# A fused sliding-window attention and GELU MLP: the first MLP product of the last two token tiles with half its columns as seven block products

## The chip, the core and the metric

The kernel runs on one core of a Trainium2 chip. The metric is the device time of one execution in microseconds; several runs are made, and their median is the time of the kernel. The engines are named as in the profile: PE is TensorE, DVE is VectorE, ACT is ScalarE, POOL is GpSimd, SP is SyncE (which here only issues transfers).

## What is computed

```python
# q, k, v: (8 batches, 8 heads, 576 positions, 64), float32
scores = (q @ k.T) / 8                      # only |i - j| <= 32 kept
x = (softmax(scores) @ v)                   # as (4608 tokens, 512)
h = x @ w_in                                # w_in: (512, 2048)
g = 0.5 * h * (1 + tanh(sqrt(2/pi) * (h + 0.044715 * h**3)))
out = g @ w_out                             # w_out: (2048, 512), result float32
```

## The kernel before

The attention output is kept in SBUF, transposed and in fp16, as `xT`: 128 partitions x 4 blocks of the 512 model columns x a ring of 1536 tokens. The MLP runs over 9 tiles `t` of 512 tokens (line 816). The attention of batch `b = t + 1` is worked in between the matmuls of tile t, so tiles 7 and 8 have no attention of their own, but for the tail of batch 7 in tile 7.

**First product** (`ffn_in`, line 525). For each of 16 columns of 128 hidden units, four matmuls of 128 x 128 weights by 512 tokens add up in one PSUM bank; `gelu` (line 550) sends the bank through the GELU on ScalarE into `gTs[t]` (fp16). The call number n is mapped to a column by `column`: n = 0, 1, 2, 3 are columns 0, 8, 1, 9, and so on. After every fourth n, `sums` (line 579) forms on VectorE four sums S1 to S4 of the GELU outputs (columns 2i, 2i + 1 with columns 8 + 2i, 9 + 2i, and the two halves of the tokens), which the second product needs. `S2` needs `S1`, `S4` needs `S2`. The first three columns of a tile are begun (three of four matmuls) at the end of the tile before (lines 930 to 932).

**Second product** (`ffn_out`, line 625). For t of 1 and up the product with `w_out` is already a Strassen-Winograd one: `WINO` (line 41) lists seven products, each of 16 matmuls of 256 columns, 112 in all, numbered i = 0 to 111. Product 0 is A11 B11 and goes over f = 0 to 7, one f for each GELU column of the lower half; product 1 is S2 T2. At the end of each product VectorE copies a bank out or adds it to what was kept (lines 653 to 671), and `ffn_last` makes the last sum; `store` issues the output, mostly on GpSimd's queue. Some products add into a bank that has just been copied out, so TensorE waits for that copy.

**Order of the work.** Every engine takes its instructions in the order in which the program issues them. The attention is placed by hand: a plan (`PLAN`, line 46, for tiles 2 to 6; `PLAN_0` and `PLAN_1` for tiles 0 and 1) says at which i which steps are visited: `s` scores and exponential, `m` the mask on VectorE, `v` the sums and the product with V and the inversion on ScalarE (with the load of a tail of V on GpSimd's queue at `v-1`), `x` the product into `xT` on VectorE; `@` names the PSUM pair, and -1 is the tail of the batch before. Ahead of the first visit ScalarE's table is loaded anew. Tile 7 has `v-1` at 5 and `x-1` at 31. `load_v` and a one-column copy that waits for the transposed keys are issued on GpSimd's queue at i = 4.

**PSUM.** Eight banks: `psM` has two (`bank(0)`, `bank(1)`), `psS` two pairs (`S0`, `S1`), `psO` two (`O`, `D`). The first product of tiles 1 and up uses banks 0 and 1, `D`, and for n = 1, 2 the pair `S0`. The tail's weights at `v-1` of tile 7 use `O` and `D`, and `D` is also the bank of n = 15.

**Copies touched.** At the end of tile 0, `ffn_out_0` (line 612) copies four banks out, those of t4 = 0, 1 on VectorE, t4 = 2, 3 on ScalarE (line 622). In tile 1 the block C11 is copied out by ScalarE, in later tiles by VectorE (line 657).

Of the kernel before, what the change touches and what calls it, by code (L numbers as in the profile page):

```python
# [9 lines left out]
FP32 = mybir.dt.float32  # L10
FP16 = mybir.dt.float16
AF = mybir.ActivationFunctionType
ALU = mybir.AluOpType
# [23 lines left out]
def cut(b):  # L37
# [5 lines left out]

PLAN = {4: "s0@0 s1@1 v-1", 16: "m0 m1 x-1", 33: "s2@0 v0@1 v1", 36: "m2", 44: "x0", 50: "x1",
        62: "s3@0 s4@1 v2", 66: "m3", 80: "x2", 84: "m4", 91: "v3", 112: "x3"}


# [4 lines left out]
          29: "w2", 33: "s-1@1 n0@0", 35: "e0", 36: "m2", 37: "k3", 38: "w5", 39: "m-1", 40: "r3@1", 43: "e1",  # L54
          46: "s3@0 v-1@1 d0", 47: "w3 e2", 48: "d1 m3", 51: "n2@0", 52: "e3 d2 d3 x-1",
          55: "u3 p0@0 p2@1 x0 x1", 56: "e4 x2 x3", 60: "c1"}
PLAN_1 = {12: "s0@0 s1@1 s2", 16: "m0 m1", 36: "m2", 45: "v0@1 v1 s-1@0", 52: "x0", 55: "x1", 62: "m-1",
          69: "s3@0 v2 v-1@1", 73: "m3", 81: "x2", 85: "x-1", 91: "v3 s4@1", 112: "x3 m4"}
PAIR_1 = {17: slice(0, 4), 40: slice(4, 8)}
# [10 lines left out]
def kernel(  # L70
# [479 lines left out]
    def gelu(t, n):  # L550
        fc = column(t, n)
        nc.scalar.activation(gTs[t][:, fc, :], phs[fc], AF.Gelu_apprx_tanh)  # L552
        if t and n % 4 == 3:
            sums(t, n // 4)

    wino = {}

    def combine_w():
# [53 lines left out]
    def ffn_out_0(t4, fc):  # L612
        new = t4 not in pys
        if new:
            pys[t4] = bank(t4) if t4 < 2 else psO.tile([128, 512], FP32, name="py3", tag="OD"[t4 % 2])
        nc.tensor.matmul(pys[t4], gTs[0][:, fc, t4 * 128:t4 * 128 + 128], w_out16[:, fc, :],
                         start=new, stop=(fc == NF - 1))
        if fc == NF - 1:
            if "yo" not in pys:
                pys["yo"] = hp.tile([128, 2, 512], FP32, name="yo2", tag="qt16")  # L620
            yo = pys["yo"][:, t4, :] if t4 < 2 else yp.tile([128, 512], FP32, name="yo", tag="yo")
            (nc.scalar.copy if t4 > 1 else nc.vector.tensor_copy)(yo, pys[t4])  # L622
            later.append((t4, yo))

    def ffn_out(t, i):

        n, blk, f = i // 16, i // 8 % 2, i % 8
        a, w, new = WINO[n]
        end = t == NT - 1
        if i % 16 == 0 and new:  # L630
            pys[n % 2] = bank((1 + n) % 2)
            if end and n == 4:
                pys["apart"] = psO.tile([128, 512], FP32, name="py2", tag="O")
        py = pys[n % 2].rearrange("p (b c) -> p b c", b=2)
        apart = end and blk and n in (4, 6)
        if a[0] == "A":
            r0, c0 = 8 * (int(a[2]) - 1) + f, 256 * (int(a[1]) - 1) + 128 * blk
            lhsT = gTs[t][:, r0, c0:c0 + 128]
        else:
            lhsT = wino[a][:, f, 128 * blk:128 * blk + 128]  # L640
        one = end and n in (4, 6)
        nc.tensor.matmul(pys["apart"][:, 0:256] if apart else py[:, blk, :], lhsT,  # L642
                         wino[w][:, f, :], start=(new and i % (8 if one else 16) == 0),
                         stop=(i % (8 if one else 16) == (7 if one else 15)),
                         skip_group_check=True)
        if i % 16 < 15:
            return
        yo, left, right = wino["yo"], slice(0, 256), slice(256, 512)
        C11, C12, C21, C22 = (yo[:, r:r + 2, c] for r in (0, 2) for c in (left, right))

        M1, U2, U3 = C21, C12, C22
        if n == 0:
            nc.vector.tensor_copy(M1, py)
        elif n == 1:
            nc.vector.tensor_tensor(U2, py, M1, op=ALU.add)
        elif n == 2:
            (nc.vector.tensor_copy if t > 1 else nc.scalar.copy)(C11, py)  # L657
            if end:
                for x in range(2):
                    store(t, x, yo[:, x, :], left, nc.sync)  # L660
        elif n == 3:
            nc.vector.tensor_tensor(U3, py, M1, op=ALU.add)
        elif n == 4:
            if not end:
                nc.vector.tensor_tensor(C22, py, U3, op=ALU.add)
            else:
                for x, part in enumerate((py[:, 0, :], pys["apart"][:, 0:256])):
                    nc.vector.tensor_tensor(C22[:, x, :], part, U3[:, x, :], op=ALU.add)
                    store(t, 2 + x, yo[:, 2 + x, :], right, nc.sync, nc.scalar)
        elif n == 5:  # L670
            nc.vector.tensor_tensor(C21, py, M1, op=ALU.add)  # L671
            for x in range(2):
                store(t, 2 + x, yo[:, 2 + x, :], *((left, nc.sync, nc.scalar) if end else ()))
# [142 lines left out]
    for t in range(NT):  # L816
        b = t + 1
        att = b < B
        if t:
            for fc in range(begun):  # L820
                ffn_in(t, fc, 3, 4, then=False)
            for fc in range(begun):
                gelu(t, fc)
            if att and b > 1:
                parts = cast_and_turn(b)
            for fc in range(begun, NF):
                ffn_in(t, fc)
                if t == 1 and fc == 3:
                    parts[0]()
                    combine(4, nc.vector)  # L830
                if t == 1 and 6 <= fc < 10:
                    cast_v(2, fc - 6)
                if t == 1 and 9 <= fc < 14:
                    parts[1](fc - 9)
                if t == 1 and fc == 8:
                    trans_tails(1, psO.tile([128, 8, 128], FP16, name="pt", tag="O"))
                if t == 2 and fc in (8, 9):
                    store(0, *later[1 if fc == 8 else 3])
                if t > 1 and fc == 8 and att:
                    pair_v(b, nc.vector.tensor_copy)  # L840
# [10 lines left out]
        for i in range(113 if t else 65):  # L851
# [3 lines left out]
            for act in plan.get(i, "").split():  # L855
# [8 lines left out]
                elif kind == "e":  # L864
                    cast_vt(1) if g == 4 else cast_v(1, g)
                elif kind == "k":
                    cast_early(1, g, (nc.vector, nc.vector))
                    if g == 2:
                        cast_tails(0, nc.gpsimd, even)
                elif kind == "t":  # L870
                    trans_tails(0, spare(at)[0], even)
                elif kind == "r":
                    trans_pair(1, g, *spare(at), copy=nc.scalar.copy if g == 2 else nc.vector.tensor_copy)
                elif kind in "np":
                    pair = psS.tile([128, 2, 512], FP32, name="ps_od", tag=f"S{at}")
                    for x in range(2):
                        if kind == "n":
                            sum_up(1, g + x, pair[:, x, :], groups[(1, g + x)])
                        else:
                            ods[g + x] = (pair[:, x, :], lts[g + x])  # L880
                            times(1, g + x, pair[:, x, :], groups.pop((1, g + x)))
                    if kind == "n":
                        n = size(1, g)
                        lts[g], lts[g + 1] = lt4[:, g, :], lt4[:, g + 1, :]
                        for x in range(2):
                            nc.scalar.activation(lts[g + x][:, 0:n], pair[:, x, 0:n], AF.Ln)
                        for x in range(2):
                            nc.scalar.activation(lts[g + x][:, 0:n], lts[g + x][:, 0:n], AF.Exp, scale=-1.0)
                elif kind == "u":
                    cast_w(wo[g], w_out16[:, 12:16, :], on_act=(3,), cs=(2, 3))  # L890
                    cast_tails(1, nc.gpsimd)
                    load_qk(2)
                elif kind == "c":
                    if g == 1:
                        B12 = combine_w()
                    combine(g, nc.vector)
                elif kind == "s":
                    score(*group(g), at)
                    if t == 1 and g == 4:
                        load_table(gelu_set)  # L900
                elif kind == "d":
                    pair_chunk(b, g, nc.vector.tensor_copy)
                elif kind == "m":
                    mask(*group(g))
                elif kind == "v":
                    bb, gg = group(g)
                    o, d = weigh(bb, gg, at)
                    ods[g] = (o, invert(bb, gg, d))
                    if t and g < 0 and b + 1 < B:
                        load_vt(b + 1)  # L910
                    if t > 1 and g == (3 if att else -1):
                        load_table(gelu_set)
                else:
                    spread(*group(g), *ods[g])
            if t == 1 and i == 30:
                cast_vt(2)
                store(0, *later[0])
# [43 lines left out]
```

## Time and profile before

| what | value |
|---|---|
| time, three runs | 300.5, 301.97, 308.7 us; median 301.97 |
| time of the profiled execution | 301.21 us |
| its span | 299.5 us |
| granted TensorE clock, mean | 0.998 |
| busy: PE, DVE, ACT, POOL | 287.0, 194.4, 194.1, 91.0 us |
| first product of tile 7 | 242.29 to 256.12 us of the span |
| second product of tile 7 | 256.12 to 269.10 us |
| first product of tile 8 | 269.10 to 282.91 us |

A row of groups gives line, engine, operation, output and inputs with their shapes, the count, the busy time in us, the mean in ns, and the idle time of the engine ahead of it with its releaser. A row of the timeline gives start and duration in us. The chain of waits follows the work that ended last back through what released it; there the matmuls stand one behind the other at the pace at which they are issued[...].

### The profile page before, as it was taken

Reading aid. Unit: us, or ns where it says so; the run is one execution under the profiler, and the core shown is the slowest. Engines: PE = TensorE matmul, PEld = TensorE weight load, DVE = VectorE, ACT = ScalarE, POOL = GpSimd, SP = SyncE. Lnnn points to the kernel's source line nnn. Section 1 sums busy time; section 2 is a strip of 40 time slices with the busy share of each in tenths; the row PEclk is TensorE's granted clock in tenths of the full one; section 3 lists DMA queues with packets and bytes.
Section 4 is the critical chain, followed back from the end, with each engine's and each line's share of the span. In section 5 each row is a group of like instructions: output and inputs, shape, how many; then the busy total and the mean of one; then the engine's idle time right before and its main releaser. Section 6 shows DMA issues by size and latency. Waiting matters only on the chain.

```text
span 299.5 us, 7127 instructions
## 1 busy us (share of the span) xinstructions
PE 287.0 (96%) x2893; PEld 179.6 (60%) x2893; DVE 194.4 (65%) x438; ACT 194.1 (65%) x308; POOL 91.0 (30%) x141
## 2 busy tenths in 40 slices
PE   7889999999899999999999999999999999999994
PEld 3534444446674488448854885478547864784583
DVE  4753577898865975867696769766876635442452
ACT  5866767779586786578566956695678666606600
POOL 3435425202656060605080606060700050016000
PEclk9999999999999999999999999999999999999999
DMA  7999999899799979998999996989694031004013
GB/s 221 266 306 382 354 286 239 230 191 205 188 213 216 244 201 178 168 136 211 176 181 151 220 171 154 146 212 174 106 167 51 3 103 39 2 4 138 2 35 105
DMA packets 116519, 50.73 MB, mean 169 GB/s; under 512 B 98008, under 2 KB 110040, under 8 KB 116487
## 3 DMA queue, kind: packets, MB, share of 16 engines
q1 hardware_dynamic: 87428, 37.88, 62.0%
q0 software_dynamic: 27936, 11.35, 25.2%
q10 hardware_dynamic: 1122, 1.06, 1.1%
q8 instruction: 22, 0.36, 0.5%
q14 instruction: 11, 0.08, 0.1%
HBM read 36.70 MB, written 9.44 MB: 154 GB/s over the span
## 4 chain that ended last, share of the span: by engine, by line
PE 64%; DMA 21%; SPq 7%; ACT 4%; DVE 2%; issue 1%; POOL 0%
PE mm L642 28%; PE mm L544 15%; PE ph L544 13%; DMA KT<-k 5%; DMA tr<-in_q_dram 4%; DMA wst<-in_moe_w_in_dram 3%; DMA wst<-in_moe_w_out_dram 3%; SPq L173 3%; DMA kt<-in_k_dram 3%; PE ps_s L435 2%; DMA vr<-in_v_dram 2%; PE ps_d L462 2%; DMA tr<-in_k_dram 2%; SPq L227 2%; PE ps_o L472 2%; SPq L175 1%
## 5 line engine op out<-in xcount | busy, mean ns | idle before, releaser
L544 PEld LDWEIGHTS <-w_in 128*128 128x128 f16 x576 | 56.1, 98 | 66.6 <-issue 0.9
L544 PE MATMUL mm<-xT,w_in 128*128 128x512 f16 x304 | 74.7, 379 | 0.4 <-DVE yo L622 0.4
L552 ACT ACTIVATE gT<-mm 128x512 f16<-128x512 f32 x76 | 45.1, 597 | 39.9 <-PE mm L544 39.2
L544 PE MATMUL ph<-xT,w_in 128*128 128x512 f16 x272 | 68.2, 379 | 0.4 <-POOL w_in L758 0.4
L606 POOL DMA_DIRECT2D out_dram<-y x55 | 32.7, 604 | 87.4 <-DVE y L671 74.4
L642 PEld LDWEIGHTS <-s 128*128 128x128 f16 x512 | 49.6, 98 | 6.8 <-issue 0.8
L587 DVE TENSOR_TENSOR s<-gT 128x512 f16<-128x512 f16 x64 | 27.2, 426 | 32.1 <-ACT gT L552 32.1
L552 ACT ACTIVATE gT<-ph 128x512 f16<-128x512 f32 x68 | 37.9, 600 | 13.3 <-PE ph L544 13.3
L642 PE MATMUL mm<-t,s 128*128 128x256 f16 x376 | 44.9, 273 | 0.7 <-ACT y L657 0.7
L642 PEld LDWEIGHTS <-gT 128*128 128x128 f16 x384 | 36.0, 98 | 6.6
L448 ACT ACTIVATE pe<-ps_s 128x960 f16<-128x960 f32 (+1 forms) x31 | 29.5, 975 | 13.6 <-PE ps_s L435 13.5
L642 PE MATMUL mm<-w_out,gT 128*128 128x256 f16 x256 | 32.8, 273 | 0.0
L95 ACT ACT_TABLE_LOAD x18 | 23.1, 1283 | 2.2 <-issue 1.9
L498 ACT ACTIVATE lt<-lt 128x480 f32<-128x480 f32 (+3 forms) x36 | 21.1, 585 | 1.1
L497 ACT ACTIVATE lt<-ps_d 128x480 f32<-128x480 f32 (+2 forms) x28 | 15.6, 556 | 9.4 <-PE ps_d L462 6.3
L457 DVE TENSOR_TENSOR pe<-pe,band 128x960 f16<-128x960 f16 x28 | 18.3, 668 | 2.7 <-ACT pe L448 2.7
L181 POOL DMA_DIRECT2D V<-in_v_dram x20 | 17.9, 913 | 0.8 <-issue 0.4
L472 PEld LDWEIGHTS <-V 128*64 128x64 f16 x520 | 13.9, 111 | 7.1 <-DVE V L191 2.4
L642 PE MATMUL mm<-t,gT 128*128 128x256 f16 x128 | 16.3, 273 | 0.0
L435 PE MATMUL ps_s<-QT,KT 64*64 64x128 f16 (+3 forms) x576 | 13.5, 216 | 1.3 <-DMA KT<-k 0.5
L853 POOL COPY after<-KL 128x1 f16<-128x1 f16 x5 | 1.7, 339 | 42.5 <-DMA KL<-kt 42.5
L435 PEld LDWEIGHTS <-KT 64*64 64x64 f16 x576 | 10.0, 106 | 7.5 <-issue 3.4
(111 smaller groups left out, 336.7 us busy)
## 6 DMA issues: line engine op xcount, KB each, us to landing
kr<-in_k_dram SPq DMA_DIRECT2D x31, 256.0 KB, 11.4
qr<-in_q_dram SPq DMA_DIRECT2D x6, 1024.0 KB, 8.1
wst<-in_moe_w_in_dram SPq DMA_DIRECT2D x7, 512.0 KB, 8.2
V<-in_v_dram POOLq DMA_DIRECT2D x20, 128.0 KB, 8.5
wst<-in_moe_w_out_dram SPq DMA_DIRECT2D x2, 1024.0 KB, 11.9
wst<-in_moe_w_out_dram SPq DMA_DIRECT2D x4, 512.0 KB
qr<-in_q_dram SPq DMA_DIRECT2D x7, 256.0 KB, 6.8
out_dram<-y POOLq DMA_DIRECT2D x6, 192.0 KB, 5.9
```

The lines of the kernel that those rows point to most:

```text
L95: nc.scalar.add_instruction(mybir.InstLoadActFuncSet(name=nc.get_next_instruction_name(), act_func_set_id=which, ins=[], outs=[]))
L181: nc.gpsimd.dma_start(V[:, c, :, :], v[b, :, 128 * c:128 * c + 128, :].rearrange("h p d -> p h d"))
L435: nc.tensor.matmul(sides[h][64 * half:64 * half + 64, 4 * n * r:4 * n * r + 4 * n].rearrange("k (j p) -> k j p", j=4)[:, :, p0 - q0:p1 - q ...
L448: nc.scalar.activation(pe, ps[:, :, 0:w], AF.Exp, scale=SCALE)
L457: nc.vector.tensor_tensor(pe, pe, m.rearrange("k (o j) p -> k o j p", o=1).broadcast_to(list(pe.shape)), op=ALU.mult)
L472: nc.tensor.matmul(o[64 * h:64 * h + 64, cols].rearrange("d (j p) -> d j p", j=4)[:, :, p0 - q0:p1 - q0], Vs[b % 2][:, slot, 2 * pr + h, : ...
L498: nc.scalar.activation(lt[:, 0:n], lt[:, 0:n], AF.Exp, scale=-1.0)
L544: nc.tensor.matmul(ph, w_in16[:, dc, fc * 128:fc * 128 + 128], xT[:, dc, t * 512 % RING:t * 512 % RING + 512], start=(dc == 0), stop=(dc = ...
L552: nc.scalar.activation(gTs[t][:, fc, :], phs[fc], AF.Gelu_apprx_tanh)
L587: nc.vector.tensor_tensor(dst, x, y, op=op)
L606: eng.dma_start(out_v[b, j, q0 + p:q0 + p + e, cols], yo[m:m + e, cols])
L642: nc.tensor.matmul(pys["apart"][:, 0:256] if apart else py[:, blk, :], lhsT, wino[w][:, f, :], start=(new and i % (8 if one else 16) == 0) ...
```

## The change

In tiles 7 and 8 the 16 columns are worked as 8 plain columns and two units A and B of four columns each (2, 3, 10, 11 and 4, 5, 12, 13). A unit's four columns, the two halves of the 512 model columns and the two halves of the tokens make a 2 x 2 block product, done with the seven products of `WINO`, each of four matmuls of 256 columns. `MIX` gives the order: a number is a plain column n, a letter with a digit a product of a unit.

The weight sums S1 to S4 of each unit are formed on GpSimd (`in_w`): S1, S2 at i = 92 of tile 6, S3, S4 at the start of tile 7. The token sums T1 to T4 are formed on VectorE (`in_x`): at the start of tile 7 for it, at i = 60 of tile 7 for tile 8. A unit uses three banks: products 0, 1, 3, 5 add up in the first, 2 has the second, 4 and 6 the third. Product 0 is copied out by VectorE; after 2 VectorE adds and ScalarE applies the GELU; 1 and 3 are copied out by ScalarE; after 3 of unit B VectorE adds the third banks of both units, and ScalarE applies the GELU to both; after 5 the GELU reads the bank; after 6 VectorE adds, the GELU follows, and then the four `sums` of the unit's columns. The output sums are fp32 in SBUF, weight and token sums fp16.

The other edits: the first visit of `PLAN` moves from i = 4 to 7; `ffn_out_0` copies t4 = 0 and 3 on ScalarE, 1 and 2 on VectorE; C11 of tile 1 is copied by VectorE.

```diff
-PLAN = {4: "s0@0 s1@1 v-1", 16: "m0 m1 x-1", 33: "s2@0 v0@1 v1", 36: "m2", 44: "x0", 50: "x1",
+PLAN = {7: "s0@0 s1@1 v-1", 16: "m0 m1 x-1", 33: "s2@0 v0@1 v1", 36: "m2", 44: "x0", 50: "x1",
...
+MIX = "3 A0 A2 B0 B2 A1 A4 B1 B4 12 A3 B3 13 A5 B5 A6 B6 14 15".split()
+UNITS = {"A": 1, "B": 2}
...
+    mixed = {}
+
+    def in_w(unit, *which):
+        if "w" not in mixed:
+            mixed["w"] = rawp.tile([128, 2, 4, 2, 256], FP16, name="wc", tag="qr")
+            mixed["A"] = rawp.tile([128, 3, 2, 256], FP32, name="sa", tag="qr")
+            mixed["B"] = rawp.tile([128, 3, 2, 256], FP32, name="sb", tag="kr")
+        i = UNITS[unit]
+        A11, A12, A21, A22 = (w_in16[:, d:d + 2, c + 256 * i:c + 256 * i + 256] for c in (0, 1024) for d in (0, 2))
+        S1, S2, S3, S4 = (mixed["w"][:, "AB".index(unit), x] for x in range(4))
+        mixed[unit, "w"] = dict(A11=A11, A12=A12, A22=A22, S1=S1, S2=S2, S3=S3, S4=S4)
+        for x in which:
+            dst, a, b, op = ((S1, A21, A22, ALU.add), (S2, S1, A11, ALU.subtract),
+                             (S3, A11, A21, ALU.subtract), (S4, A12, S2, ALU.subtract))[x - 1]
+            nc.gpsimd.tensor_tensor(dst, a, b, op=op)
+
+    def in_x(t):
+        pos = t * 512 % RING
+        B11, B12, B21, B22 = (xT[:, d:d + 2, pos + c:pos + c + 256] for d in (0, 2) for c in (0, 256))
+        xc = hp.tile([128, 4, 2, 256], FP16, name="xc", tag="q16" if t % 2 else "k16")
+        T1, T2, T3, T4 = (xc[:, x] for x in range(4))
+        mixed["x"] = dict(B11=B11, B21=B21, B22=B22, T1=T1, T2=T2, T3=T3, T4=T4)
+        for dst, a, b in ((T1, B12, B11), (T2, B22, T1), (T3, B22, B12), (T4, B21, T2)):
+            nc.vector.tensor_tensor(dst, a, b, op=ALU.subtract)
+
+    def in_step(t, unit, n):
+        i = UNITS[unit]
+        a, w, new = WINO[n]
+        key = (unit, "a" if n in (0, 1, 3, 5) else "b" if n == 2 else "c")
+        if n in (0, 2, 4):
+            if (unit, n) == ("A", 0):
+                bank_of = psO.tile([128, 512], FP32, name="pu", tag="O")
+            elif (unit, n) == ("B", 2):
+                bank_of = bank(0)
+            else:
+                if unit == "A":
+                    mixed["ps"] = psS.tile([128, 2, 512], FP32, name="pu2", tag="S1" if n == 2 else "S0")
+                bank_of = mixed["ps"][:, 0 if unit == "A" else 1, :]
+            phs[key] = bank_of.rearrange("p (h c) -> p h c", h=2)
+        ps = phs[key]
+        lhs, rhs = mixed[unit, "w"][a], mixed["x"][w]
+        for h in range(2):
+            for d in range(2):
+                nc.tensor.matmul(ps[:, h, :], lhs[:, d, 128 * h:128 * h + 128], rhs[:, d, :],
+                                 start=(n in (0, 2, 4) and h == d == 0), stop=(h == d == 1), skip_group_check=True)
+        s1, s2, s3 = (mixed[unit][:, x] for x in range(3))
+
+        def out_of(src, r, c):
+            nc.scalar.activation(gTs[t][:, 8 * r + 2 * i:8 * r + 2 * i + 2, 256 * c:256 * c + 256], src,
+                                 AF.Gelu_apprx_tanh)
+
+        def total(x, r, c):
+            nc.vector.tensor_tensor(x, ps, x, op=ALU.add)
+            out_of(x, r, c)
+
+        if n == 0:
+            nc.vector.tensor_copy(s1, ps)
+        elif n == 2:
+            total(s1, 0, 0)
+        elif n == 1:
+            nc.scalar.copy(s2, ps)
+        elif n == 3:
+            nc.scalar.copy(s3, ps)
+            if unit == "B":
+                for u in "AB":
+                    x = mixed[u][:, 2]
+                    nc.vector.tensor_tensor(x, phs[u, "c"], x, op=ALU.add)
+                for u in "AB":
+                    j = UNITS[u]
+                    nc.scalar.activation(gTs[t][:, 8 + 2 * j:10 + 2 * j, 256:512], mixed[u][:, 2], AF.Gelu_apprx_tanh)
+        elif n == 5:
+            out_of(ps, 1, 0)
+        elif n == 6:
+            total(s2, 0, 1)
+            sums(t, i)
...
-            (nc.scalar.copy if t4 > 1 else nc.vector.tensor_copy)(yo, pys[t4])
+            (nc.scalar.copy if t4 in (0, 3) else nc.vector.tensor_copy)(yo, pys[t4])
...
-            (nc.vector.tensor_copy if t > 1 else nc.scalar.copy)(C11, py)
+            nc.vector.tensor_copy(C11, py)
...
-            for fc in range(begun, NF):
+            if t > 6:
+                if t == 7:
+                    in_x(7)
+                    in_w("A", 3)
+                    in_w("B", 3)
+                    in_w("A", 4)
+                    in_w("B", 4)
+                for step in MIX:
+                    if step[0] in UNITS:
+                        in_step(t, step[0], int(step[1]))
+                    else:
+                        ffn_in(t, int(step))
+            for fc in range(begun, NF if t < 7 else 0):
                 ffn_in(t, fc)
...
+            if t == 7 and i == 60:
+                in_x(8)
+            if t == 6 and i == 92:
+                in_w("A", 1, 2)
+                in_w("B", 1, 2)
```

## Prediction

> **What bounds the kernel now.** I read the busy shares first, then TensorE's waits, the stretches of the changed stage, the chain of waits there, and last the order of time inside the stage.
>
> ```profile
> PE 287.0 (96%) x2893; PEld 179.6 (60%) x2893; DVE 194.4 (65%) x438; ACT 194.1 (65%) x308; POOL 91.0 (30%) x141
> ```
> ```profile
> PE mm L642 <- ACT y L657: 0.7, 1, 0.7
> ...
> PE ps_s L435 <- DMA KT<-k: 0.5, 2, 0.3
> ...
> PE mm L544 <- DVE yo L622: 0.4, 1, 0.4
> ```
> ```profile
> 242.29:256.12 13.83, 13.83 (x66) 6.32 (x65) 5.32 (x14) 8.63 (x15) 3.73 (x7) 1.00 0.27 76
> 269.10:282.91 13.81, 13.81 (x66) 6.32 (x65) 5.32 (x14) 8.63 (x15) 4.93 (x9) 1.00 0.27 78
> ```
> TensorE has work for 96% of the span. Its waits on others (engine, line, total, times, longest) are a few tenths each; the three shown are those that the change's small edits touch. In the two stretches (start:end, length, then busy time of PE, PEld, DVE, ACT, POOL) TensorE never rests, so there only less TensorE work, or a new wait, moves the end. VectorE has 5.3 of 13.8 us in use, but the mean hides the order in which it works:
>
> ```profile
> 244.23 0.22 PE mm L544
> 244.45 1.29 PE ph L544 x6
> 245.74 1.73 PE mm L544 x8
> ```
> ```profile
> 244.98 1.57 ACT L552 ACTIVATE gT<-ph 128x512 f16<-128x512 f32 x3
> ...
> 246.58 0.42 DVE L587 TENSOR_TENSOR s<-gT 128x512 f16<-128x512 f16 x1 [3.50 <-ACT gT L552]
> ...
> 247.04 0.42 DVE L587 TENSOR_TENSOR s<-s,gT 128x512 f16<-128x512 f16 x1
> ...
> 247.38 0.42 DVE L587 TENSOR_TENSOR s<-gT 128x512 f16<-128x512 f16 x1
> ...
> 247.72 0.42 DVE L587 TENSOR_TENSOR s<-gT,s 128x512 f16<-128x512 f16 x1
> ```
> The chain gives TensorE's pace: 1.73/8 = 0.216 us for 512 columns. Column 3 of tile 7 is finished at 245.74; its GELU is the last of the three (1.57/3, so one each 0.5) and ends at 246.55; the four sums of `sums(7, 0)` follow and let VectorE go at about 248.08. Today nothing waits for VectorE there.
>
> ```profile
> 72.08 0.90 POOL L302 CAST V<-qr 128x512 f16<-128x512 f32 x1 [16.34 <-DVE s L587]
> 72.43 0.83 DVE L587 TENSOR_TENSOR s<-gT 128x512 f16<-128x512 f16 x1
> ```
> Here, in tile 1, a GpSimd cast runs beside a sum: the sum takes 0.83 in place of 0.42 and ends 0.28 after the cast (73.26 against 72.98).
>
> [...]
>
> **Parts that save.** One 256-column matmul costs 0.109 us (the chain's 72 of line 642 in 7.86). Per tile 8 columns x 4 x 0.216 = 6.91 go, 2 units x 7 products x 4 x 0.109 = 6.10 come: -0.81, twice -1.62.
>
> The visit at 7: three more matmuls (0.33) cover the waits for the key transposes in tiles 2 and 3 (0.5 together): between 0 and -0.5, I take -0.5. It issues the scores, three exponentials, the tail's weights and one load on GpSimd's queue behind the loads of visit 4; nothing on SyncE's. Its exponentials wait for a 1.28 us table load that ends later than the moved scores, so nothing behind them is late; its mask is still due at 16.
>
> The copy of C11 in tile 1 goes from ScalarE (0.58, and 0.66 of PE idle) to VectorE (0.69), ahead of four `xT` products: -0.66 at best, 0 if tile 2's wait for transposes eats it; I take -0.5. The swap of tile 0's copies frees bank 0 earlier (0.41), but TensorE soon waits 0.74 for the pairing of V, which hangs on loads: 0 to -0.41, I take 0. Together -1.0, ends -1.6 and 0.
>
> **Parts hidden.** `in_x(7)`, four sums (0.34 apart, 0.46 where one needs the last), ends at 244.60 inside VectorE's 3.50 us of idleness; `in_x(8)` (1.5) falls into a gap of 1.05 us; the eviction behind it comes some 0.4 late, and its bank isn't added to for 1.7. `in_w(…,1,2)` comes to GpSimd's empty queue (24 us idle in tile 6) at 217.5; its four operations can hold VectorE's sums some 3 us there, which its gaps of 0.97, 0.63 and 1.90 take up; without them the pairing of V for batch 7, done at 222.2 today, would move by 3; its first product comes at 230.7. ScalarE's GELU work is unchanged (8 columns, then 8 blocks of 512), with four copies more: 4 x 0.5 = 2.0 on 8.6, room enough as a sum.
>
> **Where it stalls.** I carry the queues of tile 7 on by hand, with a PSUM eviction of 0.69 (next 0.61 later), GELU 0.60 (next 0.50 later), ScalarE copy 0.58, and 0.03 to 0.05 for a handover (246.55 to 246.58).
>
> - A0 ends at 246.18, but its copy stands behind `sums(7, 0)`: 248.08 to 248.77. A1 adds into the same bank. TensorE reaches it at 247.49 and starts at 248.82: +1.33.
> - Eviction of A2, then the copy of B0, 249.32 to 250.01; B1, reached at 249.69, starts at 250.06: +0.37. B2's eviction ends at 250.63, its GELU starts at 250.66, and the copies of A1 and B1 stand behind it, until 251.74 and 252.23: B3 +0.05.
> - The stage ends at 257.05 (before 256.12; -0.81 and +1.75).
> - At the end VectorE and ScalarE wait for each other in turn. A6 is evicted by 255.61; the sums of unit A wait for A5's GELU (256.19, behind four others), the fourth for A6's (257.19); only then comes B6's eviction, 257.69 to 258.38, its GELU at 258.41, and behind it in the queue those of columns 14 and 15, to 260.01. Five matmuls of the second product later, TensorE wants the bank of column 15 for the tail's sums: it stands from 257.60 to 260.06, 2.46 in place of 0.14 (there now 256.66 to 256.79): +2.32.
>
> Tile 7: -0.81 + 1.75 + 2.32 = +3.26. Tile 8 has the same queue; no tail there, but the matmul of f = 7 needs column 14's GELU (259.51 in tile 7's times) and loses 1.75: -0.81 + 1.75 + 1.75 = +2.69.
>
> **GpSimd against the sums.** In tile 7 only, `in_w(…,3)` and `(…,4)` start when the stores are issued, at 246.05, and the four sums alternate with four operations of D: the last ends at about 246.05 + 4D + 0.70, against 248.16 without them, so A1 and all behind it come 4D - 1.41 later. D is unknown: 0.61 is the cast's row[...]. I take 0.87[...]: +2.07[...]. GpSimd finishes at about 250, before S3 is wanted.
>
> **Sum.** -1.0 + 3.26 + 2.07 + 2.69 = +7.0 on the profiled execution's 301.21 (span 299.5), whose median of runs is 301.97: 309.0.
>
> **Rivals.** (1) GpSimd does not hold the sums: +4.95, 306.9. [...]against: the 0.83. (2) Not slower: VectorE's queue does not set A1. The place is A0's copy; it would have to start by 246.75, that is run ahead of the sums, and B6's eviction likewise; then TensorE's sum alone counts, -1.62 - 1.0, 299.4. For: 8.5 us of free VectorE time in the stretch; against: the sums start at 246.58 and are issued first. (3) TensorE cools: in A1's stall it stands 1.33 + 2.07 = 3.4 us. [...] The granted clock of before never drops in tiles 1 to 7, where no stall is as long. [...]
>
> **Numbers.** The worked case 0.52, rival 1 0.25, rival 2 0.10, rival 3 0.13. The worked case's own range is 307.9 to 310.6. The whole range, 303.5 to 312.5, takes in rivals 1 and 3 and leaves out rival 2 and mishaps beyond. 2% of 301.97 is 6.0, about what a measurement of this kernel can tell from no change: slower beyond 308.0 are nearly all of the worked case, rival 3 and a little of rival 1, 0.60; within 2%, 0.37; faster by over 2% needs more than every saving together, 0.03.
>
> **What would show it.** TensorE waiting for the copy that writes `sa` by 1.3 us in tile 8 and more in tile 7; for column 15's GELU by 2.5 at the tail in tile 7; ScalarE idle before B6's GELU with VectorE's sums in front; sums of over 0.42 beside TENSOR_TENSOR rows on POOL; no key wait at line 435. If TensorE's waits in tiles 7 and 8 sum to under 2 us, the queue argument is wrong; if tile 7's A1 waits no longer than tile 8's, the GpSimd term is.

## The result and the profile after

The changed kernel takes 321.86 us (median; 319.51 to 327.7) against 301.97: 6.4% slower, ratio 1.0639 with a 95% interval of 1.0565 to 1.0714. The direction was forecast, the size was not: 309.0 was predicted with 312.5 as the upper end. The ratios here leave out slow executions (those over 1.5% above the fastest of the same kernel); the profiled executions of all_four, on_vector and small_again are such ones, so only lengths of stages and single rows are read from them.

The profiled execution of the changed kernel took 321.86 us, its span is 320.1. First the page's busy shares and its row of the granted clock (40 slices of 8 us, in tenths):

```profile
PE 291.0 (91%) x2941; PEld 185.9 (58%) x2941; DVE 216.0 (67%) x463; ACT 196.8 (61%) x315; POOL 100.0 (31%) x149
...
PEclk9999999999999999999999999999999779997999
```

TensorE went from 96% to 91% busy, and its clock drops in three slices, at 248 to 264 us and 288 to 296: once in each of the two changed stages. TensorE's waits (engine, line, what it waited for: total, times, longest) name what came between. The line numbers are those of the changed kernel: 609 is the block products' matmul, 618 the addition `total`, 622 the copy of product 0, 673 `sums`, 578 `in_w`, 559 the plain GELU, 728 the second product, 469 the sums of the attention's weights, 442 the scores. In the versions below, added lines shift these numbers a little.

```profile
PE pu L609 <- DVE sa L618: 11.3, 4, 6.8
PE ps_d L469 <- ACT gT L559: 2.2, 1, 2.2
PE ps_s L442 <- DMA KT<-k: 2.1, 1, 2.1
PE mm L728 <- ACT gT L559: 1.5, 1, 1.5
```

The four waits on `sa` are in tiles 7 and 8, two in each. The third line is one of several in the early stretch, where waits of 1.5 on V and 1.2 on `w_out` come to it. The chain of waits at the start of tile 7 (start, us, what) shows how the longest of them is made:

```profile
247.21 2.07 ACT gT L559 x4
...
249.31 4.24 DVE s L673
...
253.58 1.10 DVE s L673 x3
254.67 0.61 DVE sa L622
...
255.38 0.70 DVE sa L618
...
256.12 1.01 PE pu L609 x4
```

The order is the one forecast (GELU of column 3, four sums, A0's copy), but the sum that should take 0.42 takes 4.24, and TensorE doesn't wait for the copy: it waits for the addition behind it. The timeline of the same stretch (start, duration, engine, line, operation, then in brackets the idle time ahead of it and its releaser) shows both reasons:

```profile
248.78 2.27 POOL L578 TENSOR_TENSOR wc<-w_in 128x512 f16<-128x512 f16 x2
249.31 4.23 DVE L673 TENSOR_TENSOR s<-gT 128x512 f16<-128x512 f16 x1 [2.04 <-ACT gT L559]
251.00 2.25 POOL L578 TENSOR_TENSOR wc<-w_in,wc 128x512 f16<-128x512 f16 x2
...
256.12 1.01 PE L609 MATMUL pu<-xT,w_in 128*128 128x256 f16 x4 [6.78 <-DVE sa L618]
...
265.28 0.60 PE L609 MATMUL pu<-xT,wc 128*128 128x256 f16 x4 [0.78 <-DVE sa L618]
```

TensorE did the eight matmuls of A0 and A2 from 248.31 on and then stood from about 249.34 to 256.12: the next in `MIX` is B0. GpSimd's four additions ran back to back from 248.78 to 253.25, and the first sum ended 0.29 after the last of them (253.54 against 253.25). The four matmuls of B0 then took 1.01; at full clock such a row is 0.60 (as in the last line), with its matmuls 0.109 apart: the granted clock was 0.50 from 254 to 258 us. That last line is B6, which waits 0.78 for A6's addition. In tile 8, where GpSimd does no additions, the same row reads:

```profile
286.97 0.42 DVE L673 TENSOR_TENSOR s<-gT 128x512 f16<-128x512 f16 x1 [3.50 <-ACT gT L559]
...
289.97 0.78 PE L609 MATMUL pu<-xT,w_in 128*128 128x256 f16 x4 [2.97 <-DVE sa L618]
```

Here the granted clock was 0.57 from 290 to 294 us.

**Where the time went.** From the start of tile 7's first product to that of tile 8's it was 26.81 us (242.29 to 269.10) and is 37.66 (245.02 to 282.68); from there to the end of the span 30.40 and 37.42.

| us | tile 7 | tile 8 and end |
|---|---|---|
| matmul work (as computed) | -0.81 | -0.81 |
| B0's wait | +6.78 | +2.97 |
| half clock after it (24 matmuls in 4.42 and 4.45, in place of 2.62) | +1.80 | +1.83 |
| B6's wait | +0.78 | +0.78 |
| wait for a GELU (2.22 less the 0.14 of before; 1.52) | +2.08 | +1.52 |
| wait for sums in the second product | | +0.36 |
| sum, against measured | 10.63 of 10.85 | 6.65 of 7.02 |

The remaining 2.73 of the span's 20.6 lie ahead of tile 7.

### The profile page after: what moved, and what is told of

Its sections match the earlier page's. It is cut to its first block, busy times and chain, and to the rows that moved or that the text cites. A ratio compares the mean times of both kernels' runs of the same rounds, so it can differ in the third digit from the quotient of the medians.

```text
span 320.1 us, 7268 instructions
## 1 busy us (share of the span) xinstructions
PE 291.0 (91%) x2941; PEld 185.9 (58%) x2941; DVE 216.0 (67%) x463; ACT 196.8 (61%) x315; POOL 100.0 (31%) x149
## 3 DMA queue, kind: packets, MB, share of 16 engines
q10 hardware_dynamic: 1122, 1.06, 1.0%
## 4 chain that ended last, share of the span: by engine, by line
PE 58%; DMA 17%; SPq 8%; ACT 8%; DVE 6%; issue 1%; POOL 0%; DVEq 0%; ACTq 0%
PE mm L728 26%; PE mm L551 12%; PE ph L551 10%; DMA wst<-in_moe_w_in_dram 5%; DVE s L673 4%; DMA tr<-in_q_dram 3%; ACT gT L559 3%; DMA kt<-in_k_dram 3%; DMA KT<-k 2%; PE pu L609 2%; SPq L180 2%; PE ps_s L442 2%; DMA wst<-in_moe_w_out_dram 2%; PE ps_d L469 2%; DMA tr<-in_k_dram 2%; SPq L234 1%
## 5 line engine op out<-in xcount | busy, mean ns | idle before, releaser
L551 PEld LDWEIGHTS <-w_in 128*128 128x128 f16 x512 | 49.6, 98 | 57.8 <-DVE w_in L222 1.1
L551 PE MATMUL ph<-xT,w_in 128*128 128x512 f16 x256 | 64.1, 379 | 0.4 <-POOL w_in L844 0.3
L551 PE MATMUL mm<-xT,w_in 128*128 128x512 f16 x256 | 63.7, 379 | 0.0
L559 ACT ACTIVATE gT<-mm 128x512 f16<-128x512 f32 x64 | 37.9, 596 | 36.2 <-PE mm L551 35.6
L673 DVE TENSOR_TENSOR s<-gT 128x512 f16<-128x512 f16 x64 | 32.5, 507 | 19.8 <-ACT gT L559 15.8
L559 ACT ACTIVATE gT<-ph 128x512 f16<-128x512 f32 x64 | 35.5, 599 | 12.5 <-PE ph L551 12.5
L188 POOL DMA_DIRECT2D V<-in_v_dram x20 | 17.9, 909 | 1.2 <-issue 1.1
L673 DVE TENSOR_TENSOR s<-s,gT 128x512 f16<-128x512 f16 x32 | 14.9, 465 | 1.1
```

What stands on the lines that cost most here:

```text
L188: nc.gpsimd.dma_start(V[:, c, :, :], v[b, :, 128 * c:128 * c + 128, :].rearrange("h p d -> p h d"))
L551: nc.tensor.matmul(ph, w_in16[:, dc, fc * 128:fc * 128 + 128], xT[:, dc, t * 512 % RING:t * 512 % RING + 512], start=(dc == 0), stop=(dc = ...
L673: nc.vector.tensor_tensor(dst, x, y, op=op)
```

## Experiments

Theory: (a) B0 lies in the second half of a two-bank tile whose first half is A2's, and waits for A2's addition although its own bank is free; (b) GpSimd's additions hold the sum ahead of it; (c) the sums stand in front of A0's copy; (d) half clock follows from the stall; (e) the two waits for GELUs come from the sums of unit A. Rivals are with each run. sums_late, tail and all_four ran on another chip than the other experiments, with the kernel before beside them. The stages, in us, each from the chain of waits of the profiled execution (small_again's isn't used); the last stage holds the last output transfer too: the span ends 3.8 to 4.1 us after VectorE's last instruction, but 4.8 after it in sums_late and 5.0 in own_bank:

| kernel | ratio to before, 95% interval | tile 7 starts | tile 7 | tile 8 to end | both |
|---|---|---|---|---|---|
| before | 1 | 242.29 | 26.81 | 30.40 | 57.2 |
| small_edits | 0.9952 [0.992, 0.9984] | 243.67 | 26.81 | 30.42 | 57.2 |
| small_again | 0.9999 [0.9974, 1.0024] | | | | |
| the change | 1.0639 [1.0565, 1.0714] | 245.02 | 37.66 | 37.42 | 75.1 |
| units_only | 1.0618 [1.0581, 1.0656] | 242.79 | 40.38 | 37.33 | 77.7 |
| w_early | 1.0595 [1.0529, 1.0661] | 245.65 | 33.82 | 37.23 | 71.1 |
| own_bank | 1.0531 [1.0479, 1.0583] | 244.11 | 37.04 | 36.15 | 73.2 |
| sums_late | 1.0157 [1.0092, 1.0221] | 241.35 | 30.37 | 34.88 | 65.3 |
| tail | 1.0382 [1.0293, 1.0471] | 240.81 | 35.39 | 34.60 | 70.0 |
| all_four | 1.0133 [1.0056, 1.0211] | 248.74 | 27.44 | 31.72 | 59.2 |
| split_sums | 1.0118 [1.0072, 1.0164] | 246.28 | 27.30 | 30.72 | 58.0 |
| on_vector | 1.0127 [1.0065, 1.019] | 250.48 | 27.88 | 30.64 | 58.5 |

**The two halves of the change.** small_edits is the kernel before with the visit, the swap of tile 0's copies and C11's copy; units_only is the changed kernel without these three.

```diff
-PLAN = {4: "s0@0 s1@1 v-1", ...
+PLAN = {7: "s0@0 s1@1 v-1", ...
...
-(nc.scalar.copy if t4 > 1 else nc.vector.tensor_copy)(yo, pys[t4])
+(nc.scalar.copy if t4 in (0, 3) else nc.vector.tensor_copy)(yo, pys[t4])
...
-(nc.vector.tensor_copy if t > 1 else nc.scalar.copy)(C11, py)
+nc.vector.tensor_copy(C11, py)
```

> The kernel before with the three small edits alone: first visit at 7, the copies of tile 0 swapped, C11 of tile 1 on VectorE. In the changed kernel tile 7 starts at 245.02, 2.7 us later than before (242.29), where -1.0 was forecast. If the small edits cause that, this kernel takes about 304.7 and tile 7 starts near 245.0. If they save what was forecast and the 2.7 is the spread of the early transfers from run to run, it takes about 301.0 and tile 7 starts near 241.3. If they do nothing, 302.0.

> The changed kernel without the three small edits, so the block products alone. If the small edits cost the 2.7 us ahead of tile 7, about 319.2. If they save 1.0, about 322.9. If the block products carry the whole change, 320 to 322 with stalls of 6.8 and 3.0 in tiles 7 and 8 as in the changed kernel.

The whole loss is in the units. The small edits gained 0.5% in one comparison and nothing in a second one on the same chip. The stages of tiles 7 and 8 stay as they were. units_only spent 2.7 us more in tile 7 than the change with the same listed waits; its clock stood lower for longer (mean over the span 0.968, in the change 0.984): the 24 matmuls from B0 on took 5.27 in place of 4.42, and the 107 of the second product behind the tail's wait of 2.21 took 13.45 in place of 11.79.

**w_early: GpSimd's additions out of tile 7.**

```diff
-                    in_w("A", 3)
-                    in_w("B", 3)
-                    in_w("A", 4)
-                    in_w("B", 4)
...
-                in_w("A", 1, 2)
-                in_w("B", 1, 2)
+                in_w("A", 1, 2, 3, 4)
+                in_w("B", 1, 2, 3, 4)
```

> The changed kernel with the weight sums S3 and S4 formed on GpSimd in tile 6 together with S1 and S2, not at the start of tile 7. Theory that GpSimd's four operations hold VectorE's first sum: that sum takes 0.42 in place of 4.23 and product B0 of tile 7 waits about 3.0 in place of 6.8, as it does in tile 8; about 318.0. Rival, that the sum waits for something else: the 4.23 stays, 321.9. Rival, that the four operations now hold VectorE in tile 6 on the path: tile 7 starts later by up to 4.

Tile 7 is 3.84 shorter. Two lines of its timeline, and one of TensorE's waits:

```profile
249.94 0.43 DVE L673 TENSOR_TENSOR s<-gT 128x512 f16<-128x512 f16 x1 [2.04 <-ACT gT L559]
...
252.95 0.60 PE L609 MATMUL pu<-xT,w_in 128*128 128x256 f16 x4 [2.97 <-DVE sa L618]
```
```profile
PE mm L728 <- DVE s L673: 1.9, 2, 1.1
```

B0 waits 2.97 in both tiles now: GpSimd's share was 6.78 - 2.97 = 3.81. That the whole stage is shorter by about the same amount is a coincidence. B0's 0.60 is the pace of full clock, so the 1.80 behind B0 is gone too; but here the clock fell behind the tail's wait of 2.21, where the change kept it: the 107 matmuls behind it took 13.10 in place of 11.79, and with the tail's own the rest of tile 7 took 13.93 in place of 12.31. The wait on sums is new: eight additions in tile 6 keep its sums late for its own second product (0.86 and 1.07 there), so the remedy gives 1.9 of its 3.8 back.

**own_bank: B0 out of the pair.**

```diff
             elif (unit, n) == ("B", 2):
                 bank_of = bank(0)
+            elif (unit, n) == ("B", 0):
+                bank_of = bank(1)
...
-                phs[fc] = bank(i) if i < 2 else phs["S"][:, n - 1, :] if i == 3 else \
+                phs[fc] = psS.tile([128, 2, 512], FP32, name="ph13", tag="S1")[:, 0, :] if t > 6 and n == 13 else \
+                    bank(i) if i < 2 else phs["S"][:, n - 1, :] if i == 3 else \
```

> The changed kernel with product 0 of unit B in a PSUM bank of a tile of its own (bank 1), not in the second half of the pair whose first half product 2 of unit A uses; plain column 13 takes a bank of the freed pair. Theory that the two halves of a pair are ordered as one tile: B0 no longer waits for the addition that evicts A2, and the first wait is that of A1 for A0's copy, which ends 0.8 earlier, with 0.87 of TensorE work done meanwhile, less about 0.4 that B1 then waits; about 1.3 less in each tile, 319.3. Rival, that B0 waits for VectorE for another reason: B0 still waits 6.8 and 3.0, 321.9.

```profile
PE pu L612 <- DVE sa L625: 6.4, 2, 5.1
...
PE pu L612 <- DVE sa L621: 1.6, 2, 0.8
```

B0 no longer waits. Line 625 is now A0's copy, line 621 the addition: TensorE goes on to A1 and stands there, 5.1 in tile 7 and 6.4 - 5.1 = 1.3 in tile 8, close to the +1.33 that the prediction worked out for A1. B6, left in its pair, keeps its two waits of 0.8. So the pair had put the wait at B0, 0.87 of matmuls earlier, and made it last until the next eviction, which ends 0.80 after A0's copy (289.93 against 289.14 in tile 8 of the change): 1.30 + 0.87 + 0.80 = 2.97. The stages gain 1.9, although the last output transfer was 1.2 slower in this execution.

**sums_late: the sums behind B2's addition.**

```diff
-        if t and n % 4 == 3:
+        if t and n % 4 == 3 and not (t > 6 and n == 3):
             sums(t, n // 4)
...
+                    if step == "B2":
+                        sums(t, 0)
```

> The changed kernel with the four sums of the plain columns 0 to 3 issued after the additions of B2, not ahead of A0's copy. Theory that VectorE's order sets the stall: B0 waits only for A2's own addition, about 0.9 in each tile in place of 6.8 and 3.0; GpSimd still holds the first sum of tile 7, but nothing waits behind it. With that the clock is not halved after the stall (1.8 in each tile): 11.6 less, 310. Rival, that VectorE's work as such is too much for the stage: the wait comes back behind the sums, at A3 or A6, and less than 6 are saved, 316 or more.

```profile
PE pu L609 <- DVE sa L618: 3.8, 4, 1.1
```

This is the largest single effect: 9.8 us in the two stages from moving four VectorE instructions, and the clock is 1.000 over the whole span. B0's wait is 1.14 in both tiles; 6.78 + 2.97 - 2 x 1.14 = 7.47 of waiting gone and 3.63 of half clock gone make 11.1; 9.8 came out, and 0.95 of the difference is the slower last transfer. The sums themselves were not wanted by anything near: at their new place one takes 1.03 beside GpSimd, and TensorE waits for none of the four. In tile 7 GpSimd's additions ran from 245.11 to 249.60; the two copies and two additions that VectorE reads from PSUM in that time took 0.69 each, as without GpSimd. So it is the sums, with both inputs in SBUF, that GpSimd held here, and not VectorE as a whole.

**tail: unit A's sums behind B6's addition.**

```diff
             total(s2, 0, 1)
-            sums(t, i)
+            if unit == "B":
+                sums(t, 1)
+                sums(t, 2)
```

> The changed kernel with the sums of unit A issued after the addition of B6, together with those of unit B, so that B6's GELU and those of columns 14 and 15 no longer stand behind them. Theory that the two queues wait for each other in turn at the end of the stage: the wait for column 15's GELU in tile 7 falls from 2.2 to some 0.5, the one in tile 8 from 1.5 to below 0.5, with up to 0.6 given back at the sums that product 1 of tile 8 reads; about 3 less, 319. Rival, that ScalarE is short of time there: the waits stay above 1.5, 321.

```profile
PE mm L730 <- DVE s L675: 0.4, 1, 0.4
```

Both waits for GELUs (2.2 and 1.5) have left the list, and this 0.4 on a sum has come. The stages gain 5.1, more than the 3 expected, because tile 8 kept its full clock after its 2.97 in this execution (1.83): B0's four matmuls took 0.60 behind it.

**all_four: w_early, sums_late and tail together, B0 and B4 in banks of their own.** Added to those three:

```diff
+            elif (unit, n) == ("B", 0):
+                bank_of = bank(1)
+            elif (unit, n) == ("B", 4):
+                bank_of = psS.tile([128, 2, 512], FP32, name="pu3", tag="S1")[:, 0, :]
...
-                phs[fc] = bank(i) if i < 2 else phs["S"][:, n - 1, :] if i == 3 else \
+                phs[fc] = psO.tile([128, 512], FP32, name="ph", tag="D") if t > 6 and n == 13 else \
+                    bank(i) if i < 2 else phs["S"][:, n - 1, :] if i == 3 else \
```

> The changed kernel with all remedies: weight sums all in tile 6, B0 and B4 in banks of tiles of their own (column 13 in D), the sums of columns 0 to 3 behind B2, those of unit A behind B6. By the queues: no wait up to column 15; ScalarE, with four copies more, ends column 15's GELU some 1.0 late at tile 7's tail and column 14's 0.4 late in tile 8, product 1 of tile 8 waits 0.3; so -0.81 + 0.9 and -0.81 + 0.7, about nothing, and the small edits' -1.4 stay: 300.5, the time of the small edits alone. If the sum of TensorE's work decides, 298.9. If a cause is not found yet, over 303.

```profile
PE mm L735 <- DVE s L680: 3.0, 3, 1.1
...
PE ps_d L469 <- ACT gT L560: 0.9, 1, 0.9
```

No wait on `sa` is left and 15.9 of the 17.9 us that the two stages had lost are back, but the ratio is 1.0133, where about 0.995 (300.5) was expected. Twelve sums stand in a row behind B6, and the last come 1.03 late for product 1 in tile 8; the tail still waits 0.9; and the other 1.9 on sums is in tile 6, from GpSimd's additions.

**split_sums and on_vector: the rest.** split_sums is all_four with two more edits: it forms only S1 and S2 of groups 1 to 3 behind B6, S3 and S4 at i = 20, and visits the tail at 9. on_vector also takes the weight sums off GpSimd and forms them on VectorE. small_again, the small edits alone once more, ran beside them.

```diff
-            sums(t, n // 4)
+            sums(t, n // 4, (1, 2) if t > 6 else (1, 2, 3, 4))
...
-                sums(t, 1)
-                sums(t, 2)
+                sums(t, 1, (1, 2))
+                sums(t, 2, (1, 2))
...
+            if t > 6 and i == 20:
+                for j in (1, 2, 3):
+                    sums(t, j, (3, 4))
...
-... {5: "v-1", 31: "x-1"} ...
+... {9: "v-1", 31: "x-1"} ...
```
```diff
-            nc.gpsimd.tensor_tensor(dst, a, b, op=op)
+            nc.vector.tensor_tensor(dst, a, b, op=op)
...
-            if t == 6 and i == 92:
+            if t == 6 and i == 97:
                 in_w("A", 1, 2, 3, 4)
-                in_w("B", 1, 2, 3, 4)
...
                     in_x(7)
+                    in_w("B", 1, 2, 3, 4)
```

> As all_four, but in tiles 7 and 8 only S1 and S2 of the column groups 1 to 3 are formed behind B6's addition, S3 and S4 at i = 20 of the second product, and the visit of the tail in tile 7 moves from i = 5 to 9. Theory (what all_four still loses in tiles 7 and 8 is twelve sums in one row ahead of product 1, 1.03, and the tail's wait for the last GELU, 0.9): both waits go, and from the start of tile 7's first product to the end of the span it takes 57.0 or less in place of 59.2; the time is about 2 us under all_four's 308.5, some 306. The waits of 0.85 and 1.07 on sums in tile 6's second product stay. Rival (the block products cost more than the sum of their matmuls, whatever waits): 58.5 or more remain without a wait over 0.5 in tiles 7 and 8.

> As split_sums, but the weight sums are formed on VectorE: unit A's at i = 97 of tile 6, unit B's at the start of tile 7; GpSimd does none of them. Theory (GpSimd's eight operations hold VectorE's sums of tile 6's first product, which then come late for its second product): the waits of 0.85 and 1.07 on sums in tile 6 go too, about 1.9 less than split_sums; from tile 7's start to the end at most 0.3 more than split_sums. With every wait gone the change keeps its -1.6 on matmuls and the -1.4 of the small edits: about 299 to 300, ratio 0.99 to 1.0, a little under small_edits. Rival (sums on VectorE only move the late queue): VectorE's eight sums make in_x or sums(7, 0) late, a wait of over 1 us appears in tile 7, and it is no faster than split_sums.

> The kernel before with the three small edits alone, beside the two others on the same chip: ratio 0.995 as before; the difference between it and on_vector is what the block products bring with all waits gone, -1.6 expected.

In split_sums no wait over 0.36 is left in the two stages, yet they take 58.0, between what theory (57.0) and rival (58.5) expected; so neither is settled. Its timeline lists three waits there: 0.19 at f = 7 of each tile and 0.36 in tile 7; two of them read:

```profile
266.43 3.65 PE L736 MATMUL mm<-t,s 128*128 128x256 f16 x32 [0.36 <-DVE y L749]
...
288.01 1.16 PE L736 MATMUL mm<-w_out,gT 128*128 128x256 f16 x9 [0.19 <-ACT gT L560]
```

Its first product takes 13.48 and 13.47 where it took 13.83 and 13.81: of the 0.81 saved, 0.35 arrives. The starts of its matmul groups show where the rest goes:

```profile
251.31 1.04 PE L614 MATMUL pu<-xc,wc 128*128 128x256 f16 x8
252.34 0.60 PE L614 MATMUL mm<-xc,wc 128*128 128x256 f16 x4
...
253.21 1.03 PE L552 MATMUL ph<-xT,w_in 128*128 128x512 f16 x4
254.27 0.60 PE L614 MATMUL pu<-xc,wc 128*128 128x256 f16 x4
```

Eight matmuls at 0.109 are 0.87; these took 1.03 from start to start, the four plain ones 1.06 in place of 0.865, and the next two groups of four 0.49 in place of 0.44: gaps of 0.16, 0.19, 0.05 and 0.05, each too short to be listed, 0.45 per tile in all. The longer two stand ahead of B1, which starts 0.06 after VectorE's copy of B0 (252.28), and of A3, which starts 0.05 after ScalarE's copy of A1 (254.22). The second product gave back 0.85 in tile 7 and 0.65 in tile 8, which the last GELU and the displaced evictions explain in part. Of the 3.6 us by which split_sums is slower than before (1.0118 of 301.30), its profile has 0.8 in the two stages and 1.9 in tile 6's waits on sums; where the rest lies is open.

on_vector had none of tile 6's waits on sums (0.85 and 1.07 in split_sums), as expected, and took 0.6 more in tile 7. Its ratio is no better; its profiled execution stood 6.5 us on a key transfer in tile 2, far ahead of any edit to tiles 6 to 8, so this run does not settle what the move to VectorE is worth. No version with the units beat the kernel before; the small edits alone are level with it or 0.5% better.

## Why the prediction was wrong, point by point

- **The step that failed is "Where it stalls".** It carried TensorE from A2 through B0 and B2 to A1 and put the first wait there, "A0's copy stands behind `sums(7, 0)` … A1 +1.33". The queue on VectorE was right: A0's copy came behind the four sums (254.67 against 249.31), and in the profile of before ScalarE's casts and GELUs of tile 1, 0.60 and 0.58 each, alternate in program order from 66.04 on. But it took B0 as free to run, since its bank was free. B0 is in the other half of A2's two-bank tile and waits for A2's addition, one eviction further on: 2.97 without GpSimd (tile 8, and w_early's tile 7) and not 1.33. B6 waits for A6 in the same way, 0.78 in each tile. own_bank shows it for B0: in another tile its wait is gone and A1's 1.3 appears; for B6 all_four does, where B4 and B6 have a tile of their own; its other edits, tried one by one, left B6's 0.78 as it was. So the order seems to come from the program's tile and not from the bank, which no run separates further; it had to be looked for in `in_step`, where both halves are cut from one tile.
- **"GpSimd against the sums": right in kind, +2.07 for 3.81.** Two terms were off. D was taken as 0.87, an assumption: the profile of before has no two-input addition on GpSimd, only casts of 0.60 to 0.93. It is 1.13 (2.27 for two). And the four were taken to alternate with four sums, an estimate from the one sum of 0.83 in tile 1: 4 x 1.13 - 1.41 would be 3.1. In tile 7 they ran back to back and the first sum got no turn among them. In tile 6 they did alternate (1.37 for a sum). It isn't that one addition there needs the one before it: in w_early S3 and S4 of unit A, of which neither needs its neighbour, alternate too (POOL, then VectorE's sums beside them). Why tile 7 differs is open.

```profile
220.55 1.33 POOL L578 TENSOR_TENSOR wc<-w_in 128x512 f16<-128x512 f16 x1
221.84 1.33 POOL L578 TENSOR_TENSOR wc<-w_in,wc 128x512 f16<-128x512 f16 x1
```
```profile
220.79 1.37 DVE L673 TENSOR_TENSOR s<-gT,s 128x512 f16<-128x512 f16 x1
222.09 1.37 DVE L673 TENSOR_TENSOR s<-gT 128x512 f16<-128x512 f16 x1
```

- **Rival 3, half clock, was given 0.13 and happened in both tiles.** It was tied to one stall, A1's 3.4 us in tile 7; that a stall lowers the clock, and by how much, the profile of before didn't show (1.00 in every stretch up to 283 us). It came behind B0's 6.78 in tile 7 (1.80) and behind the 2.97 in tile 8 (1.83), where no stall as long had been forecast. The same 2.97 was followed by a lowered clock in three tiles and by full clock in two (last section). With the long stalls gone, tiles 7 and 8 of sums_late, all_four, split_sums and on_vector ran at full clock (in each, 32 matmuls of the second product take 3.49 or 3.50 from start to start in tile 7, 24 take 2.62 in tile 8: 0.109 each).
- **The tail and tile 8's f = 7 held:** +2.32 against 2.08, +1.75 against 1.52; tail removes both by moving unit A's sums.
- **"Parts hidden" held for the change** (its list has no wait on tile 6's sums), with four additions there. With eight it no longer does (w_early, 1.9).
- **The saving of TensorE work is real and small.** -0.81 per tile is what the pace gives; the best version got 0.35 of it.
- **The small edits, -1.0 with ends -1.6 and 0:** -1.4 and 0.0 were measured (0.9952 of 302.72; 0.9999 of 301.30). The sign "no key wait at line 435" did not come: the change waits 2.1 there (line 442 now), small_edits 2.6 in two waits. The profile after starts tile 7 2.73 later. sums_late, tail, own_bank and the change issue the same instructions up to there and start it at 241.35, 240.81, 244.11 and 245.02: the early stretch, where TensorE waits for transposed keys, V and weights, spreads by 4 us between executions (the first two on another chip). So the 2.73 can't be put down to the change, and what of the ratio it makes isn't settled.

From the prediction's +7.0 to the measured +20.65 the way is 13.6: B0 and B6 in place of A1, B1 and B3, +2.00 in each tile; GpSimd in tile 7, +1.74; half clock, +3.63; the start of tile 7, +3.73; and +0.5 of small terms.

## What to carry to other kernels

Ask of each matmul not only whether its bank is free but which buffer its bank was cut from: here a matmul into the second bank of a tile waited for the read of the first (2.97 us at B0, 0.78 at B6). Before an eviction that TensorE needs soon, put nothing in VectorE's queue that isn't needed soon, least of all sums out of SBUF while GpSimd adds (here 4.23 and 1.37 for one of 0.42); moving four sums in each tile was worth 9.8 us where the products saved 0.8 per tile. A saving of under 1 us per stage that adds handovers between engines has to survive each of them: here gaps of 0.05 to 0.2 alone took half of it.

## What the runs showed of the hardware that was not expected

Four two-input GpSimd additions issued back to back kept a VectorE sum waiting through all of them (4.23 us for one of 0.42) in tile 7, while in tile 6 the two engines took turns (1.37 for a sum); VectorE's instructions on PSUM took their 0.69 beside the same additions.

The four stalls of TensorE of 5.1 to 6.8 us in tile 7 (the change, units_only, tail, own_bank) were each followed by a lowered clock: the four matmuls of B0 took 1.01 in the first three, the eight behind own_bank's 5.09 took 1.87, where eight at full clock are 1.04. Shorter ones went both ways. After 2.97 us B0's four matmuls took 0.78 (the change, tile 8), 1.01 and 1.01 (tile 8 of units_only and w_early), but 0.60, the full pace, in tile 7 of w_early and tile 8 of tail. After the tail's 2.2 us the clock fell in units_only and w_early, not in the change, own_bank and sums_late: the 107 matmuls took 13.45 and 13.10, and 11.79 in each of the other three. The first two matmuls behind it, in the change and in w_early:

```profile
270.37 0.35 PE L469 MATMUL ps_d<-pet,ones 128*64 128x384 f16 x2 [2.22 <-ACT gT L559]
```
```profile
265.54 0.50 PE L469 MATMUL ps_d<-pet,ones 128*64 128x384 f16 x2 [2.21 <-ACT gT L559]
```

What decides between the two outcomes, these runs don't show.
